# GpSimd's share of the patterns that stand in for exponentials: free copies from the base pattern, in slots of their own

## The chip, the cores and the metric

The kernel runs on one core of one Trainium2 chip. The metric is the device time of one execution in microseconds (us). The engines are named as the profile names them: TensorE (PE, its weight loads PEld), VectorE (DVE), ScalarE (ACT), GpSimd (POOL) and SyncE (SP).

## The reference

Four transformer layers run one after another over 2048 tokens of width 512 with 32 heads of width 16: A, B, A, B, each added to its input after a layer norm.

```python
def _A_ref(x, wq, wk, wv, wo, beta):      # four segments of 512 tokens
    for s in range(N):
        logits = jnp.einsum('bhqd,bhkd->bhqk', qs, ks) * scale + mask     # causal, within the segment
        p = _softmax(logits, axis=-1)
        a_dot = jnp.einsum('bhqk,bhkd->bhqd', p, vs)
        num = jnp.einsum('bhld,bhde->bhle', pq, M)                       # memory of earlier segments
        den = jnp.einsum('bhld,bhd->bhl', pq, z)[..., None] + 1e-06
        outs.append(g * (num / den) + (1.0 - g) * a_dot)
        ...
def _B_ref(x, wqkv, wo):                  # full attention, 2048 x 2048 for each head
    scores = jnp.einsum('bhqd,bhkd->bhqk', q, k) * Dh ** (-0.5)
    p = _softmax(scores, axis=-1)
    o = jnp.einsum('bhqk,bhkd->bhqd', p, v)
...
x = x + _A_ref(_layernorm(x, axis=-1), A_wq, A_wk, A_wv, A_wo, A_beta)
x = x + _B_ref(_layernorm(x, axis=-1), B_wqkv, B_wo)
x = x + _A_ref(_layernorm(x, axis=-1), A_wq, A_wk, A_wv, A_wo, A_beta)
x = x + _B_ref(_layernorm(x, axis=-1), B_wqkv, B_wo)
```

## The kernel before

Scores are made in *banks*: one block of 128 keys against 512 queries of one head fills one PSUM bank (128 x 512). A *group* is one segment of queries for four heads, with all its banks: 12 in an A layer, 64 (or a wave of 16 or 32) in a B layer. The four heads of a group sit in four sets of 32 rows of TensorE.

**Who makes the exponential.** The main loop (`attention`) goes in steps. In each step two or three banks go to ScalarE, which turns them into probabilities with one ACTIVATE (L1602; 128x1024 for two banks, 128x1536 for three); the PSUM banks are used alternately, so TensorE makes the next scores while ScalarE works. A further bank may go to VectorE instead: when `compose` gives a bank away, ScalarE's step mostly has two banks and not three (three where the base pattern comes from the spare bank `DXB`). VectorE does not compute an exponential. It scales the scores and adds a constant into unsigned 16-bit integers (`dx_first`, L1136, reading PSUM); read as bfloat16 those bits are a coarse power of two, the *base pattern*. Adding a constant distance to the bits gives a *shifted pattern* (`dx_shift`, L1213, SBUF to SBUF). TensorE adds all patterns of a bank into the output, so that their errors cancel. There are two tables of distances: `EXP_D = (0, 22, 54, 92)`, four patterns and so three shifts, and `W_D = (0, 43, 86)`, three patterns and two shifts, used with weighted copies of the values (VW). `chords` picks the table.

**Slots and batches.** Base patterns are collected into a batch of two or four banks in one slot (`dxw`, five slots of two banks; later also areas of K, Q, V, xT, woA, phk and phq that have become free, each of four banks, `dx_areas`). Because a slot may lie in such an area, the profile shows the same instruction under many names (dxw, QA, VA, KB, VB, woA, xT ...). When the batch is full, `dx_close` hands it to one of four chains (`task_dx`), which shift it, in place when the patterns have been read, and otherwise into another free slot. `dx_use` counts the users of a slot. The table of thresholds sets `wide` from 60 us on; then all four chains may run.

**GpSimd before.** From 1240 us on (`PSH` is 0 before) `pool_claim` and `pool_take` may hand a shift by 43 of the `W_D` table to GpSimd: an integer add over pairs of patterns (`pool_part`, L1264, 128x256 int32 for one bank, 128x512 for two), one step of the chain, on the batch that the chain holds. `dx_first` starts such a copy only when it has just queued a base pattern, and makes it wait for the VectorE instruction in front of that base pattern. GpSimd also clears the masked corners of A's probabilities (L1617) and makes some of the masked queries (qm, L1512).

**The order of all work is written by a planner** when the kernel is built. `Sched.add` appends every instruction to its engine's queue, notes what it must wait for, and keeps an estimated clock for each engine. Decisions compare these clocks with thresholds: how many banks of a group may go to VectorE (`TAKEN`), how far VectorE may lag (`DQ`, `DVE_LATE`), how many patterns TensorE takes in one step (`PVN`), and so on. `PIECES` is a table that changes thresholds at given times of the planned ScalarE clock. Each engine's queue runs in order.

The planner knows of one more thing: once `PSH` is set, `Sched.shared` moves a planned GpSimd instruction and a planned VectorE instruction that does not read PSUM apart, so that one begins when the other has ended.

## Time and profile before

| | |
|---|---|
| median of 3 runs | 1763.59 us (1763.25 to 1768.46) |
| the profiled execution | 1765.2 us, span 1763.5 us |
| ScalarE busy | 1721.1 us (98%) |
| TensorE busy | 1615.3 us (92%) |
| VectorE busy | 1503.3 us (85%) |
| GpSimd busy | 465.4 us (26%) |
| mean granted TensorE clock | 0.996 |

Busy time is the union of an engine's instructions. TensorE's matmuls overlap one another, so its share says little about how much room it has. In a row of a group, the numbers after the bar are busy us, mean ns of one, and idle us of the engine before them with what ended it. In a row of one line of the kernel, the three numbers are the shortest, median and longest ns. In a row of a stretch, each engine has its busy us and number of instructions, and then come the granted TensorE clock, the DMA engines' share and GB/s. A row of the timeline has its start in us, how long it took in us (the last one's end less the first one's start where several are merged), and what it is.

### The profile page before, as it was taken

The page shows a single profiled execution, that of the slowest core. Times are in us where ns is not written, and L with a number is a line of the kernel's source. Part 1 is how long each engine was busy: PE and PEld are TensorE (multiplying, and loading weights), DVE is VectorE, ACT ScalarE, POOL GpSimd, SP SyncE. Part 2 cuts the span into 40 slices and gives each one's busy share as a digit, 9 for nine tenths or more (in the row PEclk, how much of TensorE's full clock was granted, in tenths as well). Part 3 has the DMA queues.
Part 4 walks back from the last instruction along what each step waited for, and adds up shares of the span by engine and source line. Part 5 has one row for each costly group of instructions (what it writes and reads, how often), then busy time and mean ns, then how long its engine had stood idle before and what let it go on. Part 6 is the DMA issues. An engine that isn't in the chain of part 4 may idle for free.

```text
span 1763.5 us, 43148 instructions
## 1 busy us (share of the span) xinstructions
PE 1615.3 (92%) x17467; PEld 564.2 (32%) x17467; DVE 1503.3 (85%) x2962; ACT 1721.1 (98%) x1674; POOL 465.4 (26%) x911
## 2 busy tenths in 40 slices
PE   8889899999898999999989989989998899989998
PEld 4445454453224222233222332342222222222222
DVE  6677866589995999888999879768999999999997
ACT  7989998999999999999999999999999999999998
POOL 4622415110006000123000150151233334443442
PEclk9999998999999999999999999999999999999999
DMA  6121101000001000010000010110000000000000
GB/s 174 22 44 32 32 17 25 14 12 5 13 7 17 4 14 13 1 19 14 8 13 13 1 38 4 22 26 13 2 7 7 2 7 7 1 1 7 7 1 13
DMA packets 86184, 30.05 MB, mean 17 GB/s; under 512 B 78816, under 2 KB 85472, under 8 KB 85984
## 3 DMA queue, kind: packets, MB, share of 16 engines
q1 hardware_dynamic: 85984, 27.29, 7.6%
q8 instruction: 137, 2.24, 0.5%
q14 instruction: 63, 0.52, 0.1%
HBM read 6.30 MB, written 2.10 MB: 5 GB/s over the span
## 4 chain that ended last, share of the span: by engine, by line
ACT 49%; PE 26%; issue 15%; DVE 7%; POOL 2%; DMA 0%; SPq 0%; ACTq 0%; DVEq 0%; POOLq 0%
ACT pT L1602 48%; PE ps L458 26%; POOL pT L1617 2%; ACT amem L712 0%; DVE dxw L1136 0%; DMA xT<-xn 0%; DVE dxw L1213 0%; DVE KA L1735 0%; DVE KB L1136 0%; DVE QA L1136 0%; DVE rg L824 0%; DVE amem L837 0%; DVE ob L1717 0%; DVE VB L493 0%; DVE phq L715 0%
## 5 line engine op out<-in xcount | busy, mean ns | idle before, releaser
L1602 ACT ACTIVATE pT<-ps 128x1024 bf16<-128x1024 f32 (+4 forms) x1623 | 1688.7, 1191 | 27.3 <-PE ps L458 20.5
L458 PE MATMUL ps<-qm,KB 32*128 32x512 bf16 x3584 | 517.6, 384 | 67.8 <-ACT pT L1602 56.4
L458 PE MATMUL ps<-pT,VB 128*17 128x512 bf16 x2209 | 374.5, 384 | 7.0 <-ACT pT L1602 3.7
L1617 POOL TENSOR_SCALAR_AFFINE_SELECT pT<-pT 128x256 bf16<-128x256 bf16 (+2 forms) x524 | 213.1, 418 | 546.7 <-ACT pT L1602 534.0
L458 PEld LDWEIGHTS ps<-qm,KB 32*128 32x128 bf16 x3584 | 130.5, 91 | 459.2 <-ACT pT L1602 351.5
L1512 POOL TENSOR_SCALAR qm<-QB,par 128x512 bf16<-128x512 bf16 x88 | 66.8, 765 | 427.5 <-PE ps L458 389.9
L458 PEld LDWEIGHTS ps<-pT,VB 128*17 128x17 bf16 x2209 | 86.8, 87 | 237.2 <-issue 200.2
L1136 DVE TENSOR_SCALAR dxw<-ps 128x512 uint16<-128x512 f32 (+1 forms) x212 | 145.4, 697 | 4.5 <-PE ps L458 3.6
L1213 DVE TENSOR_SCALAR dxw<-dxw 128x1024 uint16<-128x1024 uint16 (+1 forms) x309 | 123.1, 408 | 3.6 <-PE ps L458 1.5
L1136 DVE TENSOR_SCALAR VA<-ps 128x512 uint16<-128x512 f32 (+1 forms) x169 | 119.1, 718 | 8.0 <-PE ps L458 6.8
L458 PE MATMUL ps<-qm,KA 32*128 32x384 bf16 (+3 forms) x1024 | 104.2, 306 | 23.6 <-ACT pT L1602 18.7
L458 PE MATMUL ps<-qm,QA 32*128 32x512 bf16 x512 | 107.1, 384 | 17.6 <-ACT pT L1602 15.7
L1136 DVE TENSOR_SCALAR QA<-ps 128x512 uint16<-128x512 f32 (+1 forms) x163 | 117.4, 733 | 4.8 <-PE ps L458 4.3
L458 PE MATMUL ps<-VA,pT 128*128 128x51 bf16 (+1 forms) x2560 | 108.0, 188 | 13.5 <-POOL pT L1617 6.6
L458 PE MATMUL ps<-dxw,VW 128*17 128x512 bf16 x422 | 104.9, 381 | 0.2 <-DVE dxw L1213 0.2
L458 PEld LDWEIGHTS ps<-VA,pT 128*128 128x128 bf16 x2560 | 85.0, 96 | 62.6 <-POOL pT L1617 31.6
L1136 DVE TENSOR_SCALAR VB<-ps 128x512 uint16<-128x512 f32 (+1 forms) x126 | 89.9, 728 | 5.0 <-PE ps L458 4.0
L1136 DVE TENSOR_SCALAR KB<-ps 128x512 uint16<-128x512 f32 (+1 forms) x116 | 89.2, 785 | 5.7 <-PE ps L458 4.7
L458 PE MATMUL ps<-pT,VA 128*17 128x512 bf16 x378 | 77.2, 384 | 1.5 <-ACT pT L1602 1.3
L458 PE MATMUL ps<-xT,wA 128*128 128x512 bf16 (+1 forms) x276 | 76.1, 381 | 1.3 <-DVE xT L673 0.9
L458 PE MATMUL ps<-dxw,VB 128*17 128x512 bf16 x256 | 74.1, 381 | 0.0
L458 PE MATMUL ps<-xT,wB 128*128 128x512 bf16 x256 | 70.6, 389 | 2.9 <-DMA xT<-xn 2.4
(333 smaller groups left out, 2626.7 us busy)
## 6 DMA issues: line engine op xcount, KB each, us to landing
out_dram<-x SPq DMA_DIRECT2D x8, 256.0 KB, 2.2
x<-in_A_x_dram SPq DMA_DIRECT2D x3, 512.0 KB, 5.0
wB<-in_B_wqkv_dram SPq DMA_DIRECT2D x1, 1536.0 KB, 11.8
xT<-xn SPq DMA_TRANSPOSE x60, 2.4
oT<-ob SPq DMA_TRANSPOSE x36, 2.4
x<-in_A_x_dram SPq DMA_DIRECT2D x4, 128.0 KB, 2.3
wA<-in_A_wq_dram SPq DMA_DIRECT2D x1, 512.0 KB, 4.4
wA<-in_A_wk_dram SPq DMA_DIRECT2D x1, 512.0 KB, 5.9
```

What stands on the lines that cost most here:

```text
L458: self.sc.add("pe", lambda e: e.matmul(out, lhsT, rhs, start=start, stop=stop, skip_group_check=True), reads=reads, banks=[(bank, "w", all ...
L1136: self.sc.add("dve", lambda e: e.tensor_scalar(d, o, SCALE * LOG2E * 128, W_C if dxs[0][:3] in self.wt else EXP_C, op0=ALU.mult, op1=ALU.add),
L1213: self.op("dve", lambda e: e.tensor_scalar(o, w, d, None, op0=ALU.add), reads=self.b_dxw[b0][:len(ents)], writes=wr, ns=(295, 425, 560, 69 ...
L1512: self.op(eng, (lambda m, q, col: lambda e: e.tensor_scalar(m, q, col, 0.0, op0=ALU.mult, op1=ALU.add))(m, q, col), reads=[bq, self.b_par] ...
L1602: self.sc.add("act", (lambda dst, src: lambda e: e.activation(dst, src, ACT.Exp, scale=SCALE))(dst, src), writes=self.b_pT[slot * 3 + i:sl ...
L1617: self.op("pool", (lambda blk, pat: lambda e: e.affine_select(blk, blk, pattern=pat, compare_op=ALU.is_ge, fill=0.0, base=0, channel_multi ...
```

## The change

- Constants: the single constant 43 (`c43`) becomes one for each distance that occurs in either table (`STEPS`, `dxc`).
- `dx_close`, when a batch is full, calls `pool_take`: for up to `PSH` patterns of the batch (but leaving at least the base), a free slot is reserved and a copy is queued in `pooled`, provided `wide` is set, the group has at least `PSH_N` banks left, GpSimd's planned backlog is at most `PSH_B`, and at least two slots are free. The remaining patterns are shifted by VectorE as before; `dx_m` holds how many those are, base included. If none is left, no chain takes the batch.
- `pool_feed` emits queued copies in the order of the queue, as long as GpSimd's planned clock is less than `PSH_A` ahead of TensorE's, at several places of each step. A copy takes up to `PSH_W` banks at once. It adds the whole distance to the base pattern, so it follows no other shift, and it waits only for its own inputs and its slot.
- The extra wait for a VectorE instruction is gone, and so are `shared`, `held` and `lock`. The planned duration of a copy is 195 + 425 ns a bank instead of 180 + 512.
- New thresholds (`PSH_W`, `PSH_A`, `PSH_B`, `TODO`, `ONE`, `MOST`, `FULLW`, `FULL_N`); `pv_some` may hold back patterns when few of a group are ready; a group closes only after its queued copies.
- `PIECES` has other values throughout. `PSH` is 2 from 380 us on, not from 1240.

```diff
@@ -20,6 +20,8 @@
...
 
+STEPS = sorted(set(EXP_D[1:] + W_D[1:]))
+
 UNIT, DXB, ACC = (0, 4), 3, 7
@@ -94,15 +94,7 @@
...
...
+    def estimate(self, op, ns, gap, tile):
         e = op.eng
@@ -124,9 +116,6 @@
...
             op.end = st + ns
-        elif port and self.lock:
-            st = self.shared(e, max(self.t[e], ready), gap)
-            op.end = self.t[e] = max(st + gap, ready + ns)
         else:
@@ -279,7 +268,7 @@
...
-    PSH, PSH_N, DXP = 0, 12, 0
+    PSH, PSH_N, PSH_W, PSH_A, PSH_B, TODO, ONE, MOST, FULLW, FULL_N = 0, 12, 2, 600, 2500, 350, 0, 2, 1, 8
@@ -291,40 +280,41 @@
...
-              (380.0, {'DX_T': 330, 'DQ': 2500, 'DMA_STEPS': 3, 'NEAR_E': 0}),
...
+              (380.0, {'DX_T': 330, 'DQ': 2500, 'PVN': 6, 'DMA_STEPS': 3, 'NEAR_E': 0, 'PSH': 2, 'PSH_N': 10, 'PSH_A': 1500, 'PSH_B': 5000, 'FULLW': 2}),
...
+              (460.0, {'CR_LOW': 2300, 'TAKEN': 1.5, 'ALTA': (1, 9, 9, 9), 'PSH_W': 1}),
...
+              (620.0, {'FILL': 0.5, 'SLACK': 150, 'REST_N': 20, 'NEAR_N': 130, 'NEAR_S': 30, 'ALT': 2}),
...
-              (740.0, {'DQ': 2500, 'DX_LATE': 1500}),
...
-              (860.0, {'BG_BANK': 200, 'AHEAD': 200, 'TAKEN': 2.7}),
...
-              (1240.0, {'NEAR': 14, 'PVN': 3, 'PVHOLE': 250, 'DMA_LATE': 300, 'PSH': 2}),
...
-              (1720.0, {'FILL_DVE': 300, 'DVE_LATE': 1500, 'GAP': 5, 'PE_B': 3, 'DX_T': 330, 'PVHOLE': 100, 'DXA': 0, 'PSH_N': 20})]
...
+              (740.0, {'BG_BANK': 0, 'DX_T': 430, 'DQ': 2500, 'DX_LATE': 1500}),
...
+              (860.0, {'MARGIN': 700, 'DVE_LATE': 1500, 'AHEAD': 200, 'TAKEN': 2.7, 'ONE': 1}),
...
+              (1400.0, {'FILL_DVE': 300, 'PSH_W': 4}),
+              (1440.0, {'PART': 2, 'FILL': 0.42, 'CR_LOW': 1500, 'DX_T': 430, 'PSH_W': 1, 'FULLW': 2}),
...
+              (1560.0, {'FIT': 3, 'BG_BANK': 500, 'PSH_B': 2500}),
+              (1600.0, {'DX_T': 480, 'PSH_B': 5000}),
...
+              (1680.0, {'CR_LOW': 2300, 'PSH_W': 2, 'PSH_A': 1000, 'FULLW': 1}),
+              (1720.0, {'GAP': 5, 'PE_B': 3, 'PVN': 8, 'DX_RES': 1, 'PSH_A': 1500})]
...
@@ -540,8 +530,9 @@
...
-        self.c43, self.b_c43 = self.nc.alloc_sbuf_tensor("c43", [P, 1], dt.int32), Buf("c43")
-        pool(lambda e: e.memset(self.c43[:, :], 43 * 65537), [self.b_c43])
+        self.dxc, self.b_dxc = self.nc.alloc_sbuf_tensor("dxc", [P, len(STEPS)], dt.int32), Buf("dxc")
+        for i, d in enumerate(STEPS):
+            pool((lambda i, d: lambda e: e.memset(self.dxc[:, i:i + 1], d * 65537))(i, d), [self.b_dxc])
@@ -1145,23 +1136,23 @@
...
-        if self.PSH and self.wide and max(self.sc.t["pool"], 0) <= self.sc.t["dve"] - (520, 1040)[k - 1]:
-            if not any(p and p["at"] < len(p["ents"]) for p in self.pooled):
-                self.pool_claim()
-            for p in self.pooled:
-                if p and p["at"] < len(p["ents"]):
-                    self.pool_part(p, k, self.sc.ops["dve"][-2])
-                    break
...
+        self.pool_feed()
...
-        self.dx_pairs.append((b, ents))
-        self.dx_todo += len(self.chords(ents)) - 1
...
+        m = len(self.chords(ents))
+        own = m - self.pool_take(b, ents, m)
+        self.dx_m[id(ents)] = own
+        if own > 1:
+            self.dx_pairs.append((b, ents))
+            self.dx_todo += own - 1
+        else:
+            self.dx_use[b] -= 1
@@ -1180,18 +1171,11 @@
...
             yield ["pair"], 0, self.DX_T * (1 if not self.dx_pairs or len(self.dx_pairs[0][1]) < 3 else 1.6)
-            if self.dx_now[k] is None:
-                self.dx_now[k] = self.dx_pairs.pop(0)
-            b, ents = self.dx_now[k]
-            for j in range(1, len(self.chords(ents))):
+            b, ents = self.dx_pairs.pop(0)
+            self.dx_now[k] = b, ents
+            for j in range(1, self.dx_m[id(ents)]):
                 if j > 1:
                     yield [("step", k)], 0, self.DX_T * (1 if len(ents) < 3 else 1.6)
-                if self.pooled[k]:
-                    job = self.pooled[k]
-                    while job["at"] < len(ents):
-                        self.pool_part(job, 2, None)
-                    self.pooled[k] = None
-                    continue
                 self.dx_shift(k, j)
@@ -1200,7 +1184,7 @@
...
-        n, last = 512 * len(ents), j == len(D) - 1
+        n, last = 512 * len(ents), j == self.dx_m[id(ents)] - 1
@@ -1218,63 +1202,52 @@
         if last:
             self.dx_use[b] -= 1
         self.dx_now[k] = b, ents
...
+
+    def pool_feed(self, g=None):
+        while self.pooled and (g is not None or self.sc.t["pool"] < self.sc.t["pe"] + self.PSH_A):
+            job = next((p for p in self.pooled if g is None or p["ents"][0][0] is g), None)
+            if job is None:
                 return
...
+            self.pool_part(job)
+
+    def pool_take(self, b, ents, m):
+
+        g, n, took = ents[0][0], len(ents), 0
+        if not self.PSH or not self.wide or g is not self.cur and g not in self.sel or len(g.banks) - g.pos < self.PSH_N:
+            return 0
+        while took < min(self.PSH, m - 1):
+            late = self.sc.t["pool"] - self.sc.t["pe"] + sum(425 * (len(p["ents"]) - p["at"]) for p in self.pooled)
+            if late > self.PSH_B or self.dx_left(n) < 2:
+                break
+            to = self.dx_pick(n)
+            self.dx_bufs.remove(to)
+            self.dx_use[to] = 1
+            self.dx_use[b] += 1
+            took += 1
+            self.pooled.append(dict(src=b, dst=to, ents=ents, at=0, j=m - took))
+        return took
+
+    def pool_part(self, job):
+
+        src, dst, ents, i0, j = (job[k] for k in ("src", "dst", "ents", "at", "j"))
+        n = min(self.PSH_W, len(ents) - i0)
         lo, hi = 512 * i0, 512 * (i0 + n)
...
+        w, o = (self.dx_space(x)[:, lo:hi].bitcast(dt.int32) for x in (src, dst))
+        wr = [x for i in range(i0, i0 + n) for x in self.dx_writes(dst, i)]
+        c = STEPS.index(self.chords(ents)[j])
+        c = bcast(self.dxc[:, c:c + 1], [[0, 256 * n]])
+        self.sc.add("pool", lambda e: e.tensor_tensor(o, w, c, ALU.add), reads=self.b_dxw[src][i0:i0 + n] + [self.b_dxc], writes=wr,
+                    ns=195 + 425 * n, gap=150 + 425 * n, name="dxp%d" % n)
+        whole = self.dx_m[id(ents)] == 1 and j == len(self.chords(ents)) - 1
         for i in range(i0, i0 + n):
             g, what, r = ents[i]
...
+            self.dx_use[dst] += 1
+            self.dxq.append((self.b_dxw[dst][i].last_write, g, what, r, dst, i, whole, j))
         job["at"] += n
         if job["at"] == len(ents):
...
+            self.pooled.remove(job)
+            self.dx_done(src)
+            self.dx_done(dst)
 
     def dx_done(self, b):
         self.dx_use[b] -= 1
@@ -1623,16 +1594,16 @@
...
         c, dxs = (2, 4)[n % 2], []
-        if self.dx_room():
+        if self.MOST and self.dx_room():
             used = {b[1] for _, b in items}
             free = self.dx_seven()
-            both = free and len(self.dx_build) % 2 == 0
-            for k in (c, DXB)[:1 + both] if both or not self.DXP else ():
+            both = free and len(self.dx_build) % 2 == 0 and self.MOST > 1
+            for k in (c, DXB)[:1 + both]:
                 f = self.dx_find(used, dxs[0][0], dxs[0][:3] in self.wt) if dxs else self.dx_find(used)
...
                     used.add(dxs[-1][2])
-            if len(dxs) == 1 and free:
+            if len(dxs) == 1 and free and not self.ONE:
                 dxs = [dxs[0][:3] + (DXB,)]
@@ -1793,7 +1764,8 @@
...
             if not due and not now and q + self.PVHOLE > max(self.pv_quad(r) for r in range(4)) and (
-                    used >= self.PVN or self.sc.t["pe"] > self.sc.t["act"] - self.PVLATE):
+                    used >= self.PVN or self.sc.t["pe"] > self.sc.t["act"] - self.PVLATE or g.fm and len(g.banks) - g.pos >= self.FULL_N
+                    and len({self.dxq[c[2]][3] for c in cand}) < self.FULLW):
                 return
@@ -1803,13 +1775,20 @@
...
-        whole = lambda: g.npv == g.total and not any(t[1] is g for t in self.dxq)
+        whole = lambda: g.npv == g.total and not any(t[1] is g for t in self.dxq) and not any(p["ents"][0][0] is g for p in self.pooled)
...
+            if must and any(p["ents"][0][0] is g for p in self.pooled):
+                self.pool_feed(g)
+                self.pv_some(g, (), True)
...
+                if any(p["ents"][0][0] is g for p in self.pooled):
+                    self.pool_feed(g)
+                    self.pv_some(g, (), True)
+                    continue
@@ -1910,12 +1888,14 @@
...
             self.compose(n, items)
+            self.pool_feed()
             self.credit(self.PE_LOW if self.low else self.PE_A if isA else self.PE_B, self.CR_LOW if self.low else self.CR_A if isA else self.CR_W * len(items) / 3 if self.wide else self.CR_B)
...
             self.background(False if split and not (self.FIT & 1 and self.wide) else None)
+            self.pool_feed()
             if self.step == 2:
```

114 lines of the change are left out of this document (26 added, 88 removed).

## The prediction

> **What bounds the kernel now.** I read the page first, then the busy time by stage, then the groups by shape, then single lines of the kernel by stage.
>
> ```profile
> span 1763.5 us, 43148 instructions
> PE 1615.3 (92%) x17467; PEld 564.2 (32%) x17467; DVE 1503.3 (85%) x2962; ACT 1721.1 (98%) x1674; POOL 465.4 (26%) x911
> ACT 49%; PE 26%; issue 15%; DVE 7%; POOL 2%; DMA 0%; SPq 0%; ACTq 0%; DVEq 0%; POOLq 0%
> L1602 ACT ACTIVATE pT<-ps 128x1024 bf16<-128x1024 f32 (+4 forms) x1623 | 1688.7, 1191 | 27.3 <-PE ps L458 20.5
> PEld ps L458 <- ACT pT L1602: 518.4, 1085, 2.3
> ```
>
> ScalarE works 98% of the span, almost all of it in the exponentials of L1602, and is idle for 27.3 us before them. TensorE looks 92% busy, but its weight loads stand 518.4 us behind ScalarE; it is elastic, except where the chain of waits runs along it (26% of the span). So the time falls in one way only: ScalarE must be given fewer banks of scores, which means that VectorE must take more. By stage (busy us of PE, PEld, DVE, ACT, POOL):
>
> ```profile
> 380.00:520.00 140.00, 132.11 (x1477) 45.22 (x1473) 135.20 (x266) 139.08 (x136) 4.83 (x6) 1.00 0.06 10
> 520.00:860.00 340.00, 313.43 (x3149) 101.49 (x3147) 292.93 (x603) 336.55 (x345) 59.34 (x146) 1.00 0.06 12
> 860.00:1000.00 140.00, 133.59 (x1132) 36.89 (x1129) 134.46 (x279) 139.39 (x138) 2.73 (x7) 1.00 0.05 9
> 1000.00:1240.00 240.00, 219.32 (x2234) 77.59 (x2234) 188.42 (x413) 236.93 (x230) 69.08 (x158) 1.00 0.10 19
> 1240.00:1480.00 240.00, 221.06 (x1972) 53.35 (x1973) 225.89 (x364) 237.68 (x224) 85.90 (x127) 1.00 0.02 6
> 1480.00:1720.00 240.00, 220.55 (x2070) 54.10 (x2066) 227.09 (x351) 238.86 (x223) 100.75 (x137) 1.00 0.01 4
> ```
>
> Between 380 and 1000 us VectorE works 562.6 of 620 us and GpSimd 66.9; from 1240 to 1720 it is 453.0 and 186.7 of 480. VectorE is full, GpSimd is idle. Only from 1000 to 1240 has VectorE room (188.42 of 240), so there something other than its time keeps banks from it.
>
> What a bank is worth, and what it costs VectorE:
>
> ```profile
> L1602 ACT ACTIVATE pT<-ps 128x1024 bf16<-128x1024 f32 x873 | 860.3, 1082 | 7.9 <-PE ps L458 5.6 <-POOL pT L1617 1.0
> L1602 ACT ACTIVATE pT<-ps 128x1536 bf16<-128x1536 f32 x591 | 854.4, 1502 | 14.7 <-PE ps L458 10.6 <-POOL pT L1617 1.1 <-POOL VB L897 0.9
> L1136 DVE TENSOR_SCALAR dxw<-ps 128x512 uint16<-128x512 f32 x206 | 138.1, 682 | 3.7 <-PE ps L458 2.9
> L1213 DVE TENSOR_SCALAR dxw<-dxw x192: 279/416/881, 379.5 to 1000.0; 128x1024 uint16<-128x1024 uint16 x179, 128x512 uint16<-128x512 uint16 x13
> L1213 DVE TENSOR_SCALAR QA<-QA x57: 415/681/694, 407.9 to 996.9; 128x2048 uint16<-128x2048 uint16 x48, 128x1024 uint16<-128x1024 uint16 x9
> L1264 POOL TENSOR_TENSOR xT<-xT,c 128x256 int32<-128x256 int32 x12 | 7.3, 612 | 10.6 <-DVE dxw L1213 5.3 <-DVE xT L1213 1.8 <-DVE VB L1136 1.8
> L1264 POOL TENSOR_TENSOR woA<-KB,c 128x512 int32<-128x512 int32 x4 | 4.2, 1039 | 7.3 <-PE ps L458 2.9 <-DVE KB L1213 2.6 <-DVE phq L1213 1.0
> ```
>
> A step whose third bank goes to VectorE saves ScalarE 1.502 − 1.082 = 0.42 us. VectorE pays 0.68 us for the base pattern (L1136), then a shift for each further pattern (L1213): 0.416 us over two banks, 0.681 over four, so 0.17 to 0.21 us a bank; I take 0.18. GpSimd pays 0.612 us for one bank's copy and 1.039 for two (L1264): dear, but in time that is empty.
>
> Banks and shifts now, by stage (VectorE busy, count):
>
> ```profile
> 380.00:520.00 140.00, 74.60 (x105) 1.00 0.06 10
> 520.00:860.00 340.00, 137.37 (x205) 1.00 0.06 12
> 860.00:1000.00 140.00, 68.88 (x104) 1.00 0.05 9
> 1240.00:1480.00 240.00, 143.59 (x195) 1.00 0.02 6
> 1480.00:1720.00 240.00, 156.55 (x199) 1.00 0.01 4
> 380.00:520.00 140.00, 45.51 (x96) 1.00 0.06 10
> 520.00:860.00 340.00, 80.75 (x172) 1.00 0.06 12
> 860.00:1000.00 140.00, 41.15 (x84) 1.00 0.05 9
> 1240.00:1480.00 240.00, 75.93 (x113) 1.00 0.02 6
> 1480.00:1720.00 240.00, 91.43 (x125) 1.00 0.01 4
> ```
>
> The first five rows are L1136, the next three L1213, the last two the copies of L1264. At 0.68 us a bank, VectorE takes 280.85/0.68 = 413 banks from 380 to 1000 us, for 167.41 us of shifts in 352 instructions; and 300.14/0.68 = 441 banks from 1240 to 1720.
>
> **The change, part by part.** Copies begin at 380 us instead of 1240, for both tables of distances, always from the base pattern into a slot of their own, up to two per bank; the copy no longer waits for an instruction of VectorE that it is then to run beside, and the plan no longer holds GpSimd and VectorE apart. What that last edit costs is the open question, because the two engines do get in each other's way:
>
> ```profile
> 1457.57 1.36 POOL L1512 TENSOR_SCALAR qm<-QB,par 128x512 bf16<-128x512 bf16 x2
> 1458.43 1.05 DVE L1213 TENSOR_SCALAR KA<-phk 128x2048 uint16<-128x2048 uint16 x1
> 1293.71 0.61 POOL L1264 TENSOR_TENSOR KA<-KB,c 128x256 int32<-128x256 int32 x1 [3.49 <-PE ps L458]
> 1292.94 1.50 DVE L1136 TENSOR_SCALAR KB<-ps 128x512 uint16<-128x512 f32 x2
> 1294.35 0.42 DVE L1213 TENSOR_SCALAR dxw<-dxw 128x1024 uint16<-128x1024 uint16 x1
> L1512 POOL TENSOR_SCALAR qm<-QB,par x62: 692/696/1241, 384.9 to 1695.9; 128x512 bf16<-128x512 bf16 x62
> ```
>
> GpSimd makes query masks (qm) until 1458.93; a shift of four banks begins at 1458.43 and takes 1.05 us instead of 0.68, so it was held for 0.37, of the 0.50 that the two lie over each other. The mask's last 0.13 us cost nothing. A mask met in the other order took up to 1241 ns instead of 696. The copies of today escape this: the one at 1293.71 runs beside base patterns, which read PSUM, and is over before the shift at 1294.35. That cover goes, for today's copies too.
>
> The price of a free copy: 352 shifts in 620 us are 0.57 a us. A copy bars 0.612 − 0.13 = 0.48 us, so it meets a shift with a chance of 0.27 and holds it 0.24 us on average: 0.06 us. VectorE's other work from SBUF (masks, normalising, transposed outputs) raises it to 0.08, an estimate. The ends are 0 (a copy falls beside base patterns again, by luck) and 0.48 (each copy holds something for its whole length). I take 0.08, because the masks are unplaced today, are as long as a copy, and their median of 696 beside a minimum of 692 says that most meet nothing. Net a copy is worth 0.18 − 0.08 = 0.10 us of VectorE.
>
> The Trainium skill, page "SBUF — State Buffer", section "Who interferes with whom", speaks against this change: the interface is an exclusive lock, held by whoever starts first for the whole instruction, while the other is blocked completely. The row of 1458.43 agrees, but for the last 0.13 us; what the whole length would make of the sum stands with the rivals.
>
> *380 to 1000 us.* Two copies for each of 413 banks would be 826, and 826 × 0.612 = 506 us would fit into GpSimd's idle 553. But each needs a slot, two slots must be free when a batch closes, the group must have ten banks left, and the backlog may not pass 5 us. I take one copy a bank, 413 (bounds 200 and 800): 41 us of VectorE freed. A bank costs 448.26/413 = 1.09 us now, about 0.95 with its copy: 43 more banks, × 0.42 = 18 us.
>
> *1000 to 1240 us.* VectorE's time doesn't decide there: 0, at most 4 us either way.
>
> *1240 us to the end.* There are 238 copy instructions to 1720 already, with 167.36 us: 0.612 a + 1.039 b over a + b = 238 gives b = 51, so 289 copied banks. GpSimd's room would hold some 750. I take 560 (bounds 400 and 750): 270 more × 0.18 = 49 us freed; but all 560, not the new ones alone, lose their cover, and with few shifts left to be met I price them at 0.05: −28. That leaves 21 us, at 0.9 a bank 23 banks, 10 us.
>
> *The rest.* More patterns mean two or three more narrow matmuls a bank; 66 banks fit into the 518 us of waiting, except in the 26% of the span where TensorE carries the chain: I take that share off the gain. The new table of thresholds can win at most ScalarE's idle 27.3 us beside what it does to the number of banks; 0, ±6. New constants in setup: a few short fills on GpSimd while ScalarE still waits for its first input, 0. No DMA is moved.
>
> Sum: (18 + 10) × 0.74 = 21 us. The profiled execution took 1765.2 us, 1.7 beyond its span and within 0.1% of the median of the runs, 1763.6. From the median: **1743 us**.
>
> **The rivals.**
> *Much faster.* Slots suffice for two copies a bank and the free copies mostly fall beside base patterns, as VectorE spends 281 of 620 us on those against 167 on shifts: 800 copies × 0.14 = 112 us, then 500 more × 0.13 = 65; 177 us at 0.95 are 186 banks, × 0.42 × 0.74 = 58 us: 1706. Against it: backlog, free slots, and patterns that TensorE must then read in time.
> *Slower: the lock.* A copy meets more than it should, since the plan does not know of it: GpSimd, once behind, runs copies one after another, and a shift that waits delays the base pattern behind it in VectorE's queue, whose PSUM bank TensorE waits for, in order, ahead of ScalarE's next scores. It decides from a mean hold of 0.18 us a copy on, where the copy's saving is gone. The two-bank copies of 1.039 us, which the table allows to 460 us and from 1680, and the four-bank ones from 1400 to 1440 bring it nearer. At 0.25 us and 970 copies: 0.07 × 970 = 68 us lost, 68 banks back to ScalarE, × 0.42 = 29 us: 1792. For it: the 1.05 us shift; against it: 696 ns as the masks' median.
> *No change.* The conditions for a copy (two free slots, ten banks left) rarely hold before 1000 us, where slots are fewest; then the first term is near 0 and the second, with its lost cover, near 5: 1760. Much the same comes out if a copy bars its whole 0.612 us: 0.57 × 0.61 × 0.31 = 0.11 us for shifts, 0.14 with the rest, so 413 × 0.04 = 17 us freed before 1000 us, and after 1240, where the price goes from 0.05 to 0.09, 49 − 50: 17/0.95 × 0.42 × 0.74 = 6 us gained, 1758. That is the rule of the Trainium skill's page "SBUF — State Buffer" taken to the letter, and the free 0.13 us speak against it.
>
> **How the numbers follow.** Forecast case (6 to 42 us gained) 0.60, much faster 0.15, no change 0.09, slower 0.16. The likeliest case alone reaches from 1722 to 1757; the range that leaves out a tenth at either side is 1708 to 1776. A measurement here can tell 0.3% (5 us) from nothing. Faster by more: 0.60 + 0.15 = 0.75; within: 0.09; slower: 0.16.
>
> **What would show it.** Right: GpSimd near 50% busy after 380 us, some 950 copied banks, most of their instructions still near 612 ns; the shifts' time from 380 to 1000 us down by a third or more; three-bank exponentials down from 591 to about 525 and two-bank ones up. The lock's price would stand in the shifts' mean, above 0.416 and 0.681. Wrong: if base patterns don't grow in number although shifts fall (something else keeps banks from VectorE), if the shifts grow longer by more than 0.18 us for each copy, or if ScalarE's idle time rises from 27.3 us.

## The result: 2.6% slower, and the profile after

The changed kernel takes 1812.47 us (median of 4 runs, 1803.83 to 1816.27) against 1766.03 for the kernel before on the same chip: a ratio of 1.0256, 95% interval 1.0213 to 1.0299, or 46 us more. The forecast was 1743 us, its range ended at 1776. The profiled execution of the changed kernel took 1803.8 us.

From the page of the changed kernel: the span, the busy time of each engine, the chain of work that ended last, the group of all exponentials.

```profile
span 1802.1 us, 44628 instructions
PE 1651.2 (92%) x17620; PEld 585.6 (32%) x17620; DVE 1505.6 (84%) x2753; ACT 1710.8 (95%) x1700; POOL 1006.2 (56%) x1727
PE 18%; DVE 14%; ACT 11%; issue 5%; POOL 4%; DMA 1%; SPq 0%; DVEq 0%; ACTq 0%; POOLq 0%
L1573 ACT ACTIVATE pT<-ps 128x1024 bf16<-128x1024 f32 (+4 forms) x1647 | 1678.1, 1125 | 76.1 <-PE ps L448 63.5
```

ScalarE has 10.3 us less work than before (1721.1 to 1710.8) but the span is 38.6 us longer: its idle time before the exponentials rose from 27.3 to 76.1 us, of which 63.5 are spent waiting for scores. The chain accounts for only 53% of the span here, against 99% before, so only its parts can be compared with one another: VectorE has 14 of 53 where it had 7 of 99, ScalarE 11 of 53 where it had 49 of 99. ScalarE no longer sets the end. VectorE's busy time is the same as before (1505.6 to 1503.3) although 209 fewer of its instructions run. The granted clock accounts for a small part of the loss: it is 0.993 in this execution (0.996 before), but 0.985 to 0.989 in the other three of the changed kernel. Executions of the kernel before that were granted 0.993 took 1765.7 to 1767.0 us, so at the same clock 37 to 38 us of the 46 are left. Over the 63 executions of the kernel before that were timed beside the experiments, the time goes from 1762 us at a clock of 0.998 to 1770 at 0.990, 1.1 us for each 0.001; the ratios below are not corrected for this, and part of it follows the holds themselves (last section).

The groups of exponentials by shape, and three of the stages (PE, PEld, DVE, ACT, POOL) of the same kernel:

```profile
L1573 ACT ACTIVATE pT<-ps 128x1024 bf16<-128x1024 f32 x1036 | 994.8, 1045 | 51.6 <-PE ps L448 45.7 <-POOL pT L1588 0.8 <-issue 0.6
L1573 ACT ACTIVATE pT<-ps 128x1536 bf16<-128x1536 f32 x460 | 650.6, 1470 | 21.9 <-PE ps L448 15.7 <-POOL pT L1588 3.0 <-POOL qm L1483 0.3
...
380.00:520.00 140.00, 130.92 (x1382) 43.72 (x1379) 132.24 (x240) 134.14 (x131) 33.17 (x37) 1.00 0.03 7
1240.00:1480.00 240.00, 223.12 (x1961) 58.97 (x1959) 217.06 (x308) 229.81 (x232) 224.43 (x324) 0.99 0.01 4
1480.00:1720.00 240.00, 216.01 (x1947) 54.37 (x1945) 221.44 (x288) 217.42 (x222) 226.88 (x368) 0.97 0.02 6
```

The change does what it says. Two-bank exponentials went from 873 to 1036, three-bank ones from 591 to 460, which is 67 banks fewer on ScalarE; GpSimd is busy 94% of the time from 1240 us on. But ScalarE, which filled all but 1.1 us of the 240 us after 1480 before the change, now stands idle for 22.6 of them.

**One place where it is lost.** The timeline of the changed kernel (start in us, duration in us, then the instruction; in brackets the engine's idle time before it and what ended it), engines one under the other:

```profile
1660.13 0.69 DVE L1127 TENSOR_SCALAR woA<-ps 128x512 uint16<-128x512 f32 x1 [0.22 <-PE ps L448]
1660.85 5.99 DVE L1197 TENSOR_SCALAR dxw<-woA 128x1024 uint16<-128x1024 uint16 x1
1666.77 0.68 DVE L1127 TENSOR_SCALAR VA<-ps 128x512 uint16<-128x512 f32 x1
...
1660.84 2.31 POOL L1239 TENSOR_TENSOR xT<-KB,dxc 128x256 int32<-128x256 int32 x4
1663.11 2.31 POOL L1239 TENSOR_TENSOR KA<-KB,dxc 128x256 int32<-128x256 int32 x4
1665.39 1.18 POOL L1239 TENSOR_TENSOR dxw<-woA,dxc 128x256 int32<-128x256 int32 x2
...
1667.50 0.60 PE L448 MATMUL ps<-qm,KB 32*128 32x512 bf16 x1 [4.01 <-DVE VA L1127]
...
1669.29 1.02 ACT L1573 ACTIVATE pT<-ps 128x1024 bf16<-128x1024 f32 x1 [4.67 <-PE ps L448]
```

A shift over two banks, 0.416 us by itself, takes 5.99 us: VectorE is *held*. It ends 0.27 us after the last of ten copies that GpSimd runs back to back. The base pattern behind it in VectorE's queue begins at 1666.77; TensorE waits 4.01 us for the PSUM bank that this base pattern reads; ScalarE then waits 4.67 us for scores. This is the chain that the prediction's slower rival described, link by link.

The lines that carry the working of the slots in the same kernel (shortest, median and longest ns, then first and last start): shifts after 1240 us, base patterns, copies.

```profile
L1197 DVE TENSOR_SCALAR VB<-KB x4: 682/927/1551, 1435.1 to 1748.5; 128x2048 uint16<-128x2048 uint16 x4
L1197 DVE TENSOR_SCALAR KB<-KB x4: 939/1073/1100, 1552.4 to 1682.1; 128x2048 uint16<-128x2048 uint16 x4
L1197 DVE TENSOR_SCALAR dxw<-phq x4: 628/734/833, 1388.9 to 1729.5; 128x1024 uint16<-128x1024 uint16 x4
L1127 DVE TENSOR_SCALAR QA<-ps x153: 652/683/1226, 302.0 to 1770.0; 128x512 uint16<-128x512 f32 x140, 128x1024 uint16<-128x1024 f32 x13
L1239 POOL TENSOR_TENSOR VB<-xT,dxc x32: 602/612/1060, 1302.0 to 1719.2; 128x256 int32<-128x256 int32 x32
```

In the two groups of four-bank shifts the medians are near 1.0 us instead of 0.681, in the group of two-bank ones 0.734 instead of 0.416; over all shifts after 1240 us they are 1.02 and 0.73. Base patterns keep their 683 ns, and most copies their 612 (807 of the 982 one-bank copies last 640 ns or less).

**Held time.** To put one number on this, I took for each VectorE instruction that overlaps a GpSimd instruction its duration beyond the median of the same line and shape where nothing overlaps it, and summed what exceeds 30 ns. Before the change this "held time" is 22.4 us (of masks and the few other GpSimd instructions), after it 91.4 us. One-bank base patterns, which read PSUM, are not among the held: in the changed kernel the 482 that copies alone overlap last 682 ns on average, and the 311 that no GpSimd instruction overlaps last 682 too.

### The profile page after: what moved, and what is told of

Same layout as the page of the kernel before. It is cut to its first block, busy times and chain, and to the rows that moved or that the text cites. A ratio compares the mean times of both kernels' runs of the same rounds, so it can differ in the third digit from the quotient of the medians.

```text
span 1802.1 us, 44628 instructions
## 1 busy us (share of the span) xinstructions
PE 1651.2 (92%) x17620; PEld 585.6 (32%) x17620; DVE 1505.6 (84%) x2753; ACT 1710.8 (95%) x1700; POOL 1006.2 (56%) x1727
## 4 chain that ended last, share of the span: by engine, by line
PE 18%; DVE 14%; ACT 11%; issue 5%; POOL 4%; DMA 1%; SPq 0%; DVEq 0%; ACTq 0%; POOLq 0%
PE ps L448 18%; ACT pT L1573 10%; DVE KB L1127 2%; DVE dxw L1197 1%; DVE VB L1127 1%; DVE xT L1127 1%; POOL KB L1239 1%; POOL dxw L1239 1%; DVE KA L1706 1%; DVE VA L1127 1%; DVE dxw L1127 1%; DMA xT<-xn 1%; POOL pT L1588 1%; DVE QA L1127 1%; DVE phk L1127 1%
## 5 line engine op out<-in xcount | busy, mean ns | idle before, releaser
L1573 ACT ACTIVATE pT<-ps 128x1024 bf16<-128x1024 f32 (+4 forms) x1647 | 1678.1, 1125 | 76.1 <-PE ps L448 63.5
L448 PE MATMUL ps<-qm,KB 32*128 32x512 bf16 x3584 | 536.1, 386 | 50.2 <-ACT pT L1573 24.7
L1239 POOL TENSOR_TENSOR dxw<-dxw,dxc 128x256 int32<-128x256 int32 (+1 forms) x211 | 147.9, 720 | 340.5 <-DVE dxw L1127 299.8
L1127 DVE TENSOR_SCALAR dxw<-ps 128x512 uint16<-128x512 f32 (+1 forms) x262 | 177.5, 697 | 7.2 <-PE ps L448 6.7
L448 PE MATMUL ps<-dxw,VW 128*17 128x512 bf16 x538 | 130.8, 382 | 2.5 <-DVE dxw L1197 1.4
L1127 DVE TENSOR_SCALAR KB<-ps 128x512 uint16<-128x512 f32 (+1 forms) x137 | 106.0, 794 | 7.4 <-PE ps L448 6.2
L1127 DVE TENSOR_SCALAR VA<-ps 128x512 uint16<-128x512 f32 (+1 forms) x147 | 104.3, 726 | 6.5 <-PE ps L448 6.1
L448 PE MATMUL ps<-dxw,VB 128*17 128x512 bf16 x363 | 101.7, 382 | 0.7 <-DVE dxw L1127 0.2
L1197 DVE TENSOR_SCALAR dxw<-dxw 128x1024 uint16<-128x1024 uint16 (+1 forms) x214 | 93.6, 447 | 6.2 <-PE ps L448 2.3
L1127 DVE TENSOR_SCALAR VB<-ps 128x512 uint16<-128x512 f32 (+1 forms) x98 | 78.2, 827 | 4.2 <-PE ps L448 4.0
```

The source lines that it names most:

```text
L448: self.sc.add("pe", lambda e: e.matmul(out, lhsT, rhs, start=start, stop=stop, skip_group_check=True), reads=reads, banks=[(bank, "w", all ...
L1127: self.sc.add("dve", lambda e: e.tensor_scalar(d, o, SCALE * LOG2E * 128, W_C if dxs[0][:3] in self.wt else EXP_C, op0=ALU.mult, op1=ALU.add),
L1197: self.op("dve", lambda e: e.tensor_scalar(o, w, d, None, op0=ALU.add), reads=self.b_dxw[b0][:len(ents)], writes=wr, ns=(295, 425, 560, 69 ...
L1239: self.sc.add("pool", lambda e: e.tensor_tensor(o, w, c, ALU.add), reads=self.b_dxw[src][i0:i0 + n] + [self.b_dxc], writes=wr, ns=195 + 42 ...
L1573: self.sc.add("act", (lambda dst, src: lambda e: e.activation(dst, src, ACT.Exp, scale=SCALE))(dst, src), writes=self.b_pT[slot * 3 + i:sl ...
```

## The experiments

Three theories were set against one another: **1**, free copies hold VectorE's SBUF-to-SBUF instructions, and the delay goes on in order to TensorE and ScalarE; **2**, the new thresholds give TensorE too many patterns; **3**, copies come late because GpSimd is full, and TensorE waits for them. "Held us" is the held time defined above. All kernels in one table, so that they can be compared; ratios are to runs of the kernel before on the same chip beside them.

| kernel | median us | ratio (95%) | held us |
|---|---|---|---|
| before | 1766.03 | 1 | 22.4 |
| after | 1812.47 | 1.0256 (1.0213 to 1.0299) | 91.4 |
| tiny_copies | 1753.05 | 0.9918 (0.9903 to 0.9932) | 21.4 |
| no_waiters | 1814.52 | 1.0262 (1.0244 to 1.0280) | 95.3 |
| paced | 1801.95 | 1.0190 (1.0161 to 1.0219) | 80.8 |
| before_free | 1777.40 | 1.0053 (1.0038 to 1.0068) | 35.4 |
| tiny_late | 1769.01 | 1.0014 (0.9999 to 1.0030) | 46.6 |
| tiny_early | 1796.51 | 1.0158 (1.0132 to 1.0185) | 69.1 |
| placed | 1962.73 | 1.1111 (1.1082 to 1.1141) | 38.5 |
| before_small | 1769.46 | 1.0008 (0.9993 to 1.0023) | 19.2 |
| old_table | 1799.96 | 1.0180 (1.0148 to 1.0212) | 49.6 |
| old_table_lock | 1800.70 | 1.0194 (1.0162 to 1.0226) | 50.3 |
| old_table_lock_paced | 1796.49 | 1.0177 (1.0143 to 1.0212) | 49.6 |
| before_delay | 1764.56 | 0.9995 (0.9979 to 1.0010) | 20.1 |
| before_delay2 | 1789.46 | 1.0132 (1.0100 to 1.0164) | 20.7 |

### tiny_copies: the same program with copies of two integers

```diff
+        o, w, c = o[:, 0:2], w[:, 0:2], bcast(self.dxc[:, 0:1], [[0, 2]])
         self.sc.add("pool", lambda e: e.tensor_tensor(o, w, c, ALU.add), ...
+        self.sc.ops["pool"][-1].copy = True
...
-            self.pv(g, what, r, self.dx_space(slot)[:, 512 * i:512 * i + 512].bitcast(dt.bfloat16), ...
+            pat = self.wB[:, 0, 0:512] if op.copy else self.dx_space(slot)[:, 512 * i:512 * i + 512].bitcast(dt.bfloat16)
+            self.pv(g, what, r, pat, ...
```

> The changed kernel with the order of every engine kept, but each GpSimd copy moves 2 integers instead of 256 a bank; TensorE still waits for it and then reads a weight tile in place of the copied pattern (so the shifted patterns of GpSimd are left out of the result). Theory 1 (copies hold VectorE's shifts at the shared SBUF interface, and the delay passes in order to TensorE and ScalarE): nearly all of the loss goes, 1740 to 1755 us, ScalarE idle before its exponentials back under 30 us. Theory 2 (the new thresholds give TensorE too many patterns, copies or not): stays at 1795 or more. Theory 3 (copies come late, since GpSimd is full after 1240 us, and TensorE waits for them): as theory 1.

From its page, engines and exponentials:

```profile
PE 1632.0 (93%) x17620; PEld 574.0 (33%) x17620; DVE 1442.4 (82%) x2753; ACT 1697.8 (97%) x1700; POOL 504.5 (29%) x1727
L1576 ACT ACTIVATE pT<-ps 128x1024 bf16<-128x1024 f32 (+4 forms) x1647 | 1665.0, 1145 | 40.0 <-PE ps L449 30.1
```

The order of work and the number of instructions are those of the changed kernel, and it beats the kernel before: 0.9918. So the new order with all its matmuls isn't too much for TensorE, and theory 2 falls. VectorE is busy 63.2 us less than in the changed kernel, close to the 70.0 us by which held time falls. The whole loss, 1.0256 − 0.9918 = 0.0338 or 60 us, hangs on the copies' length. Whether through VectorE or through TensorE's waiting for copies, this run doesn't say.

### no_waiters: full copies for which TensorE doesn't wait

The copies run in full; TensorE reads other data of the same shape in their place.

```diff
             for w in op.deps:
+                if w.copy and eng_name == "pe":
+                    continue
...
```

> The changed kernel with the order of every engine kept and the copies run in full, but TensorE reads a weight tile in place of a copied pattern and waits for no copy (the shifted patterns of GpSimd are left out of the result). Theory 1: the copies hold VectorE as before, 1790 to 1812 us. Theory 2: 1800 or more. Theory 3: the loss goes, 1740 to 1765.

From its groups and its waits, and the longest wait for copies in the changed kernel for comparison:

```profile
L1577 ACT ACTIVATE pT<-ps 128x1024 bf16<-128x1024 f32 (+4 forms) x1647 | 1678.6, 1127 | 88.3 <-PE ps L451 74.1
...
PEld ps L451 <- POOL dxw L1242: 1.0, 3, 0.5
...
PEld ps L448 <- POOL dxw L1239: 15.2, 43, 1.1
```

TensorE's waiting for copies, 28 us in the changed kernel with all its names and weight loads, falls to under 2, and the time is that of the changed kernel (1.0262 against 1.0256). Theory 3 falls. A full GpSimd could do harm in two more ways that this run leaves in place. VectorE could wait for copies: it does so for some 7 us in the changed kernel, against 4 in tiny_copies. TensorE and ScalarE could wait for GpSimd's masked corners and masked queries: 43 us, against 41 in the kernel before. Neither differs by more than 3 us, so theory 1 is left.

### tiny_early and tiny_late: where the loss arises

```diff
+        small = self.sc.t["act"] >= 1240000        # tiny_late; tiny_early: < 1240000
+        if small:
+            o, w, c = o[:, 0:2], w[:, 0:2], bcast(self.dxc[:, 0:1], [[0, 2]])
...
```

> The changed kernel, the same order; the copies planned from 1240 us on move 2 integers a bank (and TensorE reads a weight tile in their place, so their patterns are left out), the earlier ones run in full. Theory 1 with one price everywhere (0.85 us of time for each us that VectorE is held, as from the runs with small copies and with all copies: 59 us for 70 us): VectorE is held about 24 us more than with small copies, before 1240 us, so 1753 + 20 = 1773. Rival, that only a GpSimd that is full makes the loss (rows of copies after 1240 us): 1753 to 1758.

> The counterpart: the copies planned before 1240 us are the small ones (their patterns are left out), the later ones run in full. Theory 1 with one price everywhere: 46 us of holds remain, 1753 + 39 = 1792. The rival: nearly all of the loss remains, 1808 to 1812.

With only the early copies in full (tiny_late) the kernel is 0.0096 above tiny_copies, 17 us; with only the late ones in full (tiny_early) 0.0240, 42 us. The two add up to 59 of the 60 us. The changed kernel's copies by stage (GpSimd busy, count) show most of them late:

```profile
380.00:1000.00 620.00, 168.41 (x241) 1.00 0.06 11
1000.00:1240.00 240.00, 52.19 (x86) 1.00 0.08 16
1240.00:1810.00 570.00, 501.54 (x739) 0.98 0.02 5
```

Per us of held time the early part costs 17/25.2 = 0.67 us, the late part 42/47.7 = 0.88.

### paced: a copy waits for the VectorE instruction that the plan has just finished

```diff
+        done = next((d for d in reversed(self.sc.ops["dve"]) if d.end <= op.end - ns), None)
+        if done is not None and all(w.eng != "dve" or w.idx < done.idx for w in op.deps):
+            op.deps = [w for w in op.deps if w.eng != "dve"] + [done]
+            done.emit = True
```

> The changed kernel, the same order, with one wait more: a copy starts only when VectorE has finished the last instruction that the plan has ended by then, so that GpSimd cannot run on through a row of copies while a shift is held. Theory 1: the three long holds (5.7, 5.6 and 2.0 us) and the 11 us of ScalarE's idle time behind them go, the short holds stay: 1790 to 1803. Theory 2: no change, 1805 to 1815. Theory 3: GpSimd has yet another wait, slower, 1815 or more.

Two groups of shifts after 1240 us in this kernel:

```profile
L1197 DVE TENSOR_SCALAR dxw<-woA x4: 553/788/1281, 1355.5 to 1731.3; 128x1024 uint16<-128x1024 uint16 x3, 128x512 uint16<-128x512 uint16 x1
L1197 DVE TENSOR_SCALAR VB<-KB x4: 862/1046/2032, 1443.5 to 1748.4; 128x2048 uint16<-128x2048 uint16 x4
```

The long holds are gone: no instruction is held for more than 1.35 us, against 5.7 in the changed kernel. The many short ones stay (80.8 us of 91.4), and so does most of the loss (1.0190). The three long holds of the changed kernel, shifts of 5.99, 5.97 and 2.73 us, put 11 us of idle time in front of ScalarE. Pacing wins about that by the ratios (0.0066, 12 us), but the two intervals overlap a little, so this gain is not clear of the noise. The rest of the loss is the ordinary case.

### before_free: the kernel before without its wait

The plan is unchanged, still moving GpSimd and VectorE apart; only the wait at run time, which a copy has for the VectorE instruction in front of a base pattern, goes.

```diff
-                    deps=[sync] if sync is not None else [], ns=180 + 512 * n, gap=170 + 512 * n, name="dxp%d" % n)
+                    deps=[sync] if sync is not None else [], ns=180 + 512 * n, gap=170 + 512 * n, name="dxp%d" % n, loose=sync)
...
+        if loose is not None:
+            need = [w for w in dep_ops[1:] if w.eng == "dve" and not w.is_dma]
+            op.deps = [w for w in op.deps if w.eng != "dve"]
+            if need:
+                op.deps.append(max(need, key=lambda w: w.idx))
```

> The kernel before, the same order, without the extra wait that lets a copy start only beside a base pattern: its 308 copied banks start as soon as their input is there. Theory 1: they lose their cover, at 0.06 us a copied bank 18 us of VectorE are lost, and the time rises by 5 to 15 us, to 1770 to 1780. Theories 2 and 3: no change, 1762 to 1768.

Four-bank shifts after 1240 us in this kernel, and the first of the groups in the kernel before:

```profile
L1219 DVE TENSOR_SCALAR KB<-VB x12: 678/694/1097, 1290.7 to 1697.0; 128x2048 uint16<-128x2048 uint16 x12
L1219 DVE TENSOR_SCALAR xT<-KB x9: 683/694/1219, 1350.7 to 1763.2; 128x2048 uint16<-128x2048 uint16 x9
```

```profile
L1213 DVE TENSOR_SCALAR KB<-VB x12: 680/693/717, 1288.1 to 1685.0; 128x2048 uint16<-128x2048 uint16 x12
```

The wait alone is worth 0.0053, 9 us: without it the longest shift of the group KB<-VB goes from 717 to 1097 ns, held time rises by 13.0 us and ScalarE's idle time from 27.3 to 36.2. So with no other part of the change, dropping the cover costs time, 0.7 us for each us held (0.5 to 0.9 by the ratio's interval).

### before_small: what the covered copies cost

```diff
+        o, w, c = o[:, 0:2], w[:, 0:2], bcast(self.c43[:, 0:1], [[0, 2]])
```

> The kernel before, the same order, its copies moving 2 integers a bank instead of 256 (the rest of those patterns is left out, TensorE reads what stood in the slot). Theory 1: placed beside base patterns the copies held nobody, so nothing changes: 1761 to 1768. If a copy cost its share of the 0.06 us even when placed, 308 of them would give back 10 us or more: 1750 to 1757.

No difference (1.0008, 0.9993 to 1.0023), and held time 19.2 against 22.4 us. A one-bank copy of 0.612 us that waits until a base pattern of 0.682 us begins costs nothing that can be measured. The cover that the change gave up was complete, as far as can be measured.

### before_delay and before_delay2: a delay on VectorE with GpSimd left alone

212 short instructions, one behind each shift after 1240 us, that the plan doesn't know of.

```diff
+                eng_obj.memset(self.junk[:, 5 * (nth % 8):5 * (nth % 8) + 5], 0.0)       # before_delay
+                eng_obj.tensor_reduce(self.junk[:, nth % 40:nth % 40 + 1], self.zero[:, :], ...)   # before_delay2
```

> The kernel before, the same order, its copies as they are; behind each of its 213 shifts after 1240 us VectorE clears five words that nobody reads, which the plan does not know: a known delay of VectorE without any conflict at the interface, some 0.06 to 0.15 us each, 13 to 32 us in all (the trace will say). Theory 1, in the form that any unplanned us of VectorE costs 0.7 to 0.9 us, as the holds did: the time rises by 0.7 to 0.9 of the delay. Rival, that VectorE's delays are mostly taken up (the 0.33 us a us of the prediction) and that holds are dear for another reason: by a third of it.

> As before_delay, whose small clears vanished in the overlap of neighbouring instructions (62 ns each, but only 11 ns later per shift): in their place a sum over 128 constant words, from SBUF but without the shared interface, behind each of the 212 shifts after 1240 us; an added delay of some 0.1 us each, 20 to 30 us in all. Theory 1 (any unplanned us of VectorE costs 0.7 to 0.9 us): 15 to 27 us more, 1781 to 1793. Rival (VectorE's delays are mostly taken up, holds are dear for another reason): 7 to 10 us more, 1773 to 1777.

The added groups, of the first and of the second kernel, and the second one's engines:

```profile
L236 DVE MEMSET junk<- 128x5 f32 x212 | 13.1, 62 | 0.0
```

```profile
L236 DVE TENSOR_REDUCE junk<-zero 128x1 f32<-128x128 bf16 x212 | 58.9, 278 | 0.0
PE 1634.1 (91%) x17467; PEld 568.8 (32%) x17467; DVE 1537.8 (86%) x3174; ACT 1729.0 (97%) x1674; POOL 463.7 (26%) x911
```

The first is inconclusive: a clear of 62 ns vanishes in the overlap of neighbouring instructions (the next one starts 72 ns before the shift's end where it started 83 ns before it), so hardly 2 us of delay were added. The second adds 34.5 us of VectorE's busy time (1503.3 to 1537.8) and 22 us to the kernel's median (1767.60 to 1789.46), 0.63 us for each (0.51 to 0.84 by the ratio's interval). Held time stays at 20.7 us, so GpSimd has no part in it: an unplanned delay on VectorE is enough. That it costs more than half of itself is the second half of theory 1.

### placed: each copy waits out the VectorE work that it would meet by the plan

After planning, a copy that would overlap a VectorE instruction working from SBUF waits for its end, up to 1.5 us behind its planned time; else for the last such instruction before it.

```diff
+            for d in port:
+                if d.start >= at + long:
+                    break
+                if d.end <= op.start or d.end <= at and not self.behind(d, op):
+                    wait = d
+                elif late < 1500 and not self.behind(d, op):
+                    wait, at = d, max(at, d.end)
```

> The changed kernel in full, the same order; a copy whose planned time meets a VectorE instruction of the SBUF interface waits until that instruction has ended (at most 1.5 us behind its plan, and never where that could close a circle of waits), any other copy waits for the last such instruction before it. Theory 1: the holds on VectorE fall from 91 us in all to 40 or less and the time to 1765 to 1785; if copies then come too late for TensorE, its waits for GpSimd's patterns rise above their 18 us and eat part of it, 1785 to 1800. If theory 1 were wrong: 1805 or more.

Its waits:

```profile
PEld ps L452 <- POOL dxw L1243: 91.7, 101, 3.6
PE ps L452 <- POOL dxw L1243: 55.2, 65, 3.3
ACT pT L1616 <- PE ps L452: 206.1, 248, 3.9
```

Held time falls to 38.5 us, as expected, but the kernel is 11% slower, where 1765 to 1800 us were expected: now TensorE waits for copies, and ScalarE 206.1 us for TensorE. The wait of theory 3, small in the changed kernel (28 us), appears once copies are pushed back. The granted clock is lower too, 0.941 to 0.949; at 1.1 us for each 0.001, an estimate that goes far beyond the clocks it was taken from, that is some 50 of the 196 us. As a repair it fails, and it says nothing on what held time costs.

### old_table, old_table_lock and old_table_lock_paced: other thresholds, and the planner's rule

`old_table` is the changed kernel with the thresholds of before; `old_table_lock` puts `shared`, `held` and `lock` back into the planner; `old_table_lock_paced` adds the wait of `paced`, on the last finished VectorE instruction that works from SBUF.

```diff
-    PIECES = [ ... the new values ... ]
+    PIECES = [ ... the values of before ... ]
# old_table_lock also
+        elif port and self.lock:
+            st = self.shared(e, max(self.t[e], ready), gap)
+            op.end = self.t[e] = max(st + gap, ready + ns)
```

> The changed code with the table of thresholds of the kernel before, as it stands (copies from 1240 us on only, both kinds of distances, mostly two banks at once); the planner does not know that a copy and a VectorE instruction of the SBUF interface exclude each other. Theory 1: two-bank copies of 1.03 us hold longer, 25 to 40 us of holds after 1240 us, and the time is 1785 to 1805. If the new table were to blame (theory 2): 1765 to 1775.

> As old_table, but with the planner's rule of the kernel before put back, which plans copies and such VectorE instructions apart (no wait is added). Theory 1: VectorE is held less, 5 to 20 us after 1240 us, and what is left is in the plan: 1770 to 1787, below old_table by 10 us or more. Theory 2: both the same within 5 us.

> As old_table_lock, the same order, and each copy waits at run time for the last VectorE instruction of the SBUF interface that the plan has ended before it. The two runs before it showed that planning them apart does not keep them apart (50 us of holds either way). Theory 1: the wait carries the plan to the chip, holds fall from 50 towards 30 us in all, the time to 1775 to 1790. If the drift between the engines' real and planned times is as large as the copies themselves, the wait only delays copies: 1795 to 1810. Theory 2 (table): 1800.

A four-bank shift after 1240 us in the first and in the second of them:

```profile
L1196 DVE TENSOR_SCALAR VB<-xT x5: 676/1105/1528, 1469.3 to 1727.3; 128x2048 uint16<-128x2048 uint16 x5
```

```profile
L1209 DVE TENSOR_SCALAR VB<-KB x4: 696/969/1506, 1487.0 to 1554.9; 128x2048 uint16<-128x2048 uint16 x4
```

`old_table` came out as theory 1 expected. `old_table_lock` did not: theory 1 expected fewer holds and 1770 to 1787 us, but planning the two engines apart without a wait changes neither the holds (49.6, 50.3) nor the time (1.0180, 1.0194). That the engines don't run on time to within a shift's length would explain it; it was not measured. Adding a wait doesn't lower the holds either (49.6), and why stays open. One ground that was not tested is size: two-bank copies of 1.039 us don't fit beside one base pattern of 0.682. These three also run a table that was fitted to another mechanism, so their times don't price one part of the change; what they show is that the slowdown doesn't come from the new table alone. Nor do holds alone account for them: `old_table` holds VectorE 27 us longer than the kernel before and gives ScalarE 5 us less to do, and it is 32 us slower, more than a us for each us held. Its clock, 0.980 to 0.989, makes some 10 us of that by the 1.1 us above; the rest is open.

## Why the prediction was wrong, point by point

- **ScalarE bounds the kernel, and banks taken from it are worth 0.42 us: right in kind, somewhat too high.** Where copies are short, 67 fewer banks mean 23.3 us less busy time on ScalarE (1721.1 to 1697.8), 0.35 us a bank, and the kernel is faster.
- **The number of banks: right by two errors.** 66 more were forecast for VectorE, 43 of them from 380 to 1000 us. By the shapes in the traces, the banks of base patterns rose by 75 (1062 to 1137; an instruction can cover two), but not there. That the total is near 66 is luck. Base patterns by stage in the kernel before, and then base patterns and shifts in tiny_copies, where no hold blurs the times:

```profile
380.00:1000.00 620.00, 280.85 (x412) 1.00 0.06 11
1240.00:1810.00 570.00, 320.89 (x421) 1.00 0.02 5
```

```profile
380.00:1000.00 620.00, 285.95 (x422) 0.99 0.07 12
1240.00:1810.00 570.00, 350.57 (x438) 1.00 0.02 5
380.00:1000.00 620.00, 124.54 (x243) 0.99 0.07 12
1240.00:1810.00 570.00, 52.93 (x97) 1.00 0.02 5
```

  From 380 to 1000 us the shifts give back 167.41 − 124.54 = 43 us. That is near the forecast's 41 by luck: 252 banks at the full 0.17 us, and not 413 at 0.10. And only 11 more banks come of it (425 to 436; the prediction had reckoned 413 from busy time), not 43. The freed time is not spent: tiny_copies leaves VectorE busy 61 us less than before (1503.3 to 1442.4). So VectorE's time was not the only thing that kept banks from it in that stage; which threshold or slot does is not settled. After 1240 us 55 banks come (502 to 557), where 23 were forecast.
- **The price of a free copy: right.** 0.08 us, later 0.05, were forecast; (91.4 − 21.4)/1188 copied banks = 0.06; with tiny_late and tiny_early it is 25.2/357 = 0.07 for the early copies and 47.7/831 = 0.06 for the late ones, of which the three long holds are 13 us. Their number was off, early too high and late too low: by their shapes, 252 banks are copied before 1000 us (forecast 413) and 850 of the 1188 after 1240 us (forecast 560). The sketch of the port was right as well: a shift waits for the copy that runs, base patterns for nothing; the three long holds were not in it.
- **The step that failed: "Net a copy is worth 0.18 − 0.08 = 0.10 us of VectorE".** It sets a saving and a hold against each other in one currency, VectorE's time, and turns the difference into banks at 0.42 × 0.74 / 0.95, so 0.33 us of kernel time for each us. A saving can go that way, since the planner sees it and can deal out banks. A hold does not: the order is fixed when the kernel is built, the planner doesn't know of the hold, and no bank goes back to ScalarE for it. It arrives as a delay of the base pattern behind, of TensorE, of ScalarE. The runs give its price: 0.85 us of kernel time for each us held from tiny_copies to after (59/70.0), 0.81 from tiny_copies to paced, 0.70 in before_free, 0.63 for the plain delay of before_delay2. Not 0.33. The forecast's own holds were 413 × 0.08 + 560 × 0.05 = 61 us, and it priced them at 20 us of time; measured are 70 us of holds for 60 us of time.
- **The size of the gain.** With copies that hold nothing the forecast's own terms give (74/0.95 + 49/0.9) × 0.42 × 0.74 = 41 us, tiny_copies shows 15. The banks saved 23.3 us of ScalarE's time; 12.7 went into idle time before the exponentials (27.3 to 40.0).
- **The sum anew:** −15 us, and 70 us held at 0.70 to 0.85, so +34 to +44; measured +46. Of the 67 us between the forecast's −21 and this, 40 lie in the price of the holds and 26 in the smaller gain (41 forecast, 15 shown). The upper rate is taken from the same pair of runs and so closes the sum by construction; the lower comes from a kernel without the change.
- **The slower rival had the mechanism and the wrong threshold.** Hold, base pattern, PSUM bank, TensorE, ScalarE: the timeline shows each link. But it was to decide "from a mean hold of 0.18 us a copy on". By the rates above the gain of 15 us is gone at 15/(1188 × 0.85) = 0.015 us a copy, or 0.018 at 0.70. The measured 0.06 was over that from the start, so at the measured price it was the likeliest course; its 0.16 rested on the wrong threshold. The sign that the prediction named for it, ScalarE's idle time rising from 27.3 us, is the one that came; the first sign, three-bank exponentials falling, came too and proved nothing.
- **The rule that was weighed.** The Trainium skill, page "SBUF — State Buffer", section "Who interferes with whom", says that whoever issues first keeps the shared ports for its whole instruction. The trace agrees within 0.13 us, except in the three long holds, where copies that began after the shift went ahead of it. The prediction's reading of the rule was sound; what it made of the time was not.

**Still open:** why the price of a held us lies at 0.63 in one place, at 0.88 in another and above 1 in `old_table` (the clock may be part of it: tiny_late was granted 0.9935 at the median, tiny_early 0.986, and at 1.1 us for each 0.001 both prices would come out near 0.8; this was not tested); why pacing did nothing under the old table; what keeps VectorE's 61 us from being used.

## What to carry to other kernels

When the order of work is fixed at build time, time saved and time lost on one engine are not the same currency: a saving is worth what the planner makes of it, an unplanned delay on a nearly full in-order engine goes through to the end, here at 0.6 to 0.9 of its length. Price a wait taken away by the delays that it lets in, one by one, at that rate, and not by the mean of the engine's time. In this kernel a copy on GpSimd was free beside VectorE where it started with, and was shorter than, work that reads PSUM; such cover is part of the kernel, and an edit that removes it has to find another.

## What the runs showed of the hardware that was not expected

A held instruction doesn't always go after one copy. Of 180 in the changed kernel that began while a copy ran, 165 waited for that copy alone, but three stood behind a whole run of copies, up to ten back to back (5.99 us for a shift of 0.416). How the next copy got ahead of a shift that was already waiting is not shown. Making each copy wait for a VectorE instruction ended these runs.

The longest holds went with a lower TensorE clock. In the two holds of almost 6 us, TensorE stood idle for 4.5 and 4.0 us, and the granted clock was 0.5 for 6.8 us, from 1495.4 and from 1666.1 us on. Behind the hold of 2.73 us, with 1.8 us idle, it stayed at 1. The kernel before has no such stretch between 287 and 1761 us. Two stretches of 3.4 us in the changed kernel (from 788.9 and 1454.5 us) stand beside idle times of 0.8 and 1.3 us, so these figures don't give a threshold.

On VectorE an instruction of 62 ns, put between two others, delayed the next one by only 11 ns at the median, while one of 278 ns delayed it by 194: neighbours overlap, and a short one is all but free.
